# A spectral filter and a two-layer network on one core: all steps of the pieces placed anew, VectorE's half of the last operand sum at step 28 of its block in place of 21, and other steps for the loads of x

## The chip, the cores and the metric

The kernel runs on one core of a Trainium2 chip. The metric is the device time of one execution in microseconds; the time of a kernel is the median over its runs. Five engines run side by side, each with its own queue of instructions that it takes in order: TensorE (PE: matmuls; PEld: its weight loads), VectorE (DVE), ScalarE (ACT), GpSimd (POOL) and SyncE (SP). POOL and SP here mostly issue DMAs. Engines wait for each other by semaphores. One execution of the kernel before was profiled; all times of instructions below come from it.

## The reference

The first part multiplies each of 8 sequences (3008 positions, 256 channels) by a filter in the frequency domain; the second part is a two-layer network with a leaky rectifier whose slope is learned for each hidden unit.

```
batch, seq, dim = (8, 3008, 256)
n_tokens, d_model, d_ff = (24064, 256, 2048)
X = np.fft.rfft(x, axis=1)
F = (filt_r + 1j * filt_i)[None, :, :]
y = np.fft.irfft(X * F, n=x.shape[1], axis=1)
h = y.reshape(24064, 256) @ w_in
g = np.maximum(h, 0.0) + alpha * np.minimum(h, 0.0)
out = g @ w_out
```

## The kernel before

**The transform.** 3008 is 47 x 64. Each sequence b goes through four kinds of pieces, all built from matmuls with small constant matrices in fp16. The data are turned between them by way of DRAM, since the sums run over other indices.

- `load_x(b, c)`: four chunks c of x, two halves each, are loaded by DMAs that POOL issues (L170); they also convert to fp16. The tiles have four buffers.
- `piece_a` (16 a sequence): one matmul (L211), evicted by ScalarE to asb. `save_a` writes a chunk to a_dram (SP, L216) and `turn_a` reads it back turned to `at` (SP, L223).
- `piece_b` (12): two matmuls (L231), then two multiplications by the filter on VectorE: ww (L234) and uu (L235). Two DMAs from POOL then add ww, with its halves swapped, to uu (L237). These are the first kind of exchange.
- `piece_c` (12): two matmuls on uu (L249), evicted by ScalarE to v. `turn_c` writes a quarter of v to v_dram (SP, L258), `load_z` reads it back turned to zt (SP, L267).
- `piece_d` (16): four matmuls (L274), evicted to yT, the network's input.

Sequence 0 has its own way at the start (class `First`): its turns are done by TensorE, with `piece_t` (L352) in place of the way through v_dram. `neg` (L626) and `swapped` (L630) prepare the filter for the other sequences, and `combine` (L669 to L677) makes sums of the second layer's weights, in tw_s, which holds transform constants for sequence 0 before that.

**The network.** The tokens are cut into 48 blocks of 512 (some 384). For each block `up` runs 16 times: two matmuls with the first layer's weights (L498) into hps; after each second one ScalarE evicts a pair of hidden groups to gtb (L506), VectorE computes the negative part (L509, two) and adds it (L685, in `settle`). One `up` is a **step**, so block n covers the steps 16n to 16n + 15, and there are 768.

The second layer comes 17 steps later (LAG), spread evenly between the steps. Ordinary blocks use `eight` (L537): 64 matmuls of 256 columns. The blocks in FAST (the even ones from 8 on, here "split blocks") use `seven` (L559), a scheme with seven products of half-size operands in place of eight. It needs sums of quarters of gtb, made by `sums(w, h)` for half h of the hidden groups: w = 1 and 2 on VectorE to ss (L518, L520); w = 3 and 4 as accumulating DMAs from POOL onto gtb (L524), the second kind of exchange; w = 6 on VectorE, in place (L526). w = 6 with h = 1 and w = 4 with h = 0 are the two halves of the last operand sum; both are read by the last of the seven products. `late` holds VectorE's last additions and the stores, which SP issues (L467).

**What sets the order.** The order on every engine is written out by hand. The tables at the head of the file say at which step each piece is issued: STEPS_A to STEPS_D the pieces of sequences 4 to 7, FIRST those of 1 to 3, each plus p = 96 (b - 1); STEPS_T and STEPS_E the rest of sequence 0; STEPS_N `neg`; STEPS_F the move of a half of twi_s and then `swapped`; STEPS_K `combine`; STEPS_X and STEPS_Q the loads of x for the next sequence (STEPS_Q: two halves of four chunks, plus p). SUMS (TAIL near the end) holds (step in the block, w, h). BANKS says which of two PSUM banks each piece of the transform takes, in the order of issue. In a step the order is: late work, sums, pieces of the plan, `settle`, `up`, then the second layer's matmuls that are due:

```
for b, w, h in ahead.pop(step, ()):
    ...
    b.sums(w, h)
for fn, args in plan.pop(step, ()):
    fn(*args)
settle()
blk.up(j)
while todo and done < (step - LAG) / 16:
```

`turn_a` stands one step (sequences 1 and 2, in four parts) or four steps (the others) after the last `piece_a`; `turn_c` one step after each third `piece_c`.

Of the kernel before, what the change touches and what calls it, by code (L numbers as in the profile page):

```python
# [19 lines left out]
DFF = 2048  # L20
NH = 32
BANKS = (
    "010101010101010101010101010101001010010110010010101010101010100101001010010101010101010100101010"
    "101010101010101010101001010101001011010101011010110110101101010101010101101001011010101101010010"
    "101101010011010101101010101010101010110010101010101101001000101001010101010101010101010101010110"
    "101010101011010010010101101010101010101010101010101010010101101010110100100010100101010101010101"
    "01010101010101101010101101001110101010101010101010101010"
)
STEPS_A = (-84, -81, -77, -76, -65, -59, -58, -58, -56, -53, -52, -51, -50, -48, -46, -43)
STEPS_B = (-21, -15, 4, 6, 13, 21, 25, 27, 32, 40, 54, 55)  # L30
STEPS_C = (2, 10, 16, 19, 24, 33, 35, 46, 62, 63, 70, 70)
STEPS_D = (89, 89, 90, 91, 92, 94, 95, 98, 100, 101, 105, 113, 118, 125, 144, 147)
STEPS_T = (0, 0, 2, 2, 13, 17, 19, 21, 21, 35, 40, 43)
STEPS_E = (6, 6, 7, 11, 23, 27, 29, 29, 53, 54, 55, 56)
STEPS_N = (24, 29, 35, 40)
STEPS_F = (20, 16, 22, 28, 34)
STEPS_K = (118, 121, 128, 133, 144)
STEPS_X = ((20, 27, 42, 52), (107, 109, 113, 126))
STEPS_Q = (-28, -18, -8, -3, 1, 9, 15, 23)
FIRST = (  # L40
# [12 lines left out]
)  # L53
FAST = frozenset((8, 10, 12, 14, 16, 18, 20, 22, 24, 26, 28, 30, 32, 34, 36, 38, 40, 42, 43, 44, 45))
SUMS = ((9, 1, 0), (10, 3, 0), (16, 2, 0), (17, 1, 1), (17, 3, 1), (19, 2, 1), (20, 4, 0), (21, 6, 1))
TAIL = ((13, 1, 0), (13, 3, 0), (18, 1, 1), (18, 3, 1), (18, 2, 0), (18, 2, 1), (20, 4, 0), (21, 4, 1))
LAG = 17
AF = mybir.ActivationFunctionType
OP = mybir.AluOpType

# [41 lines left out]
def kernel(  # L102
# [514 lines left out]
    def put(step, fn, *args):  # L617
        plan.setdefault(step, []).append((fn, args))

    for i in range(12):  # L620
        ev = both[i % 2] if i < 4 else (on_dve, on_act)[i // 8]
        put(STEPS_T[i], f0.piece_t, 4 + i, ev)
        put(STEPS_E[i], f0.piece_d, 4 + i, ev)

# [6 lines left out]

    put(STEPS_F[0], lambda: nc.gpsimd.dma_start(out=twi_s[64:128], in_=twx_s[64:128]))
    for i in range(4):
        put(STEPS_F[1 + i], swapped, 6 * i, 6 * i + 6)
        put(STEPS_N[i], neg, 6 * i, 6 * i + 6)
    for b in range(1, NB):
        p = 96 * (b - 1)
        f = Fft(b)
        steps_a, steps_b, steps_c, steps_d = FIRST[b - 1] if b < 4 else (STEPS_A, STEPS_B, STEPS_C, STEPS_D)
        for i in range(16):  # L640
# [3 lines left out]
        if b + 1 < NB:  # L644
            for c in range(4):
                if b < 3:
                    put(STEPS_X[b - 1][c], load_x, b + 1, c)
                else:
                    for h in range(2):
                        put(p + STEPS_Q[2 * c + h], load_x, b + 1, c, (h,))  # L650
        quarters, later = (4, 1) if b < 3 else (1, 4)
# [27 lines left out]
    for n in range(5):  # L679
        put(STEPS_K[n], combine, n)  # L680
    owed = []
# [8 lines left out]
    for n, (p, t0, tn, _) in enumerate(blocks):  # L690
        old, blk = blk, Block(n, p, t0, tn)
        if blk.fast:
            for at, w, h in SUMS if n < 39 and n - 1 not in FAST else TAIL:
                ahead.setdefault(16 * n + at, []).append((blk, w, h))
        for j in range(16):
# [9 lines left out]
            blk.up(j)  # L705
            while todo and done < (step - LAG) / 16:
                try:
# [41 lines left out]
```

## Time and profile before

| what | us |
|---|---|
| median of 3 runs (777.71, 778.01, 780.72) | 778.01 |
| the profiled execution | 778.49 |
| its span, first to last instruction | 776.7 |
| TensorE busy (98% of the span) | 759.6 |
| VectorE busy (89%) | 691.0 |
| ScalarE busy (78%) | 606.1 |
| POOL busy (34%) | 264.7 |

The granted TensorE clock is 0.997 over the span. The span is cut into 40 equal slices (19.4 us each); TensorE is 90% busy or more in all but the first two and the last, and the DMA engines' share is given below it in tenths:

```profile
PE   7899999999999999999999999999999999999998
...
DMA  9996858666997679886797869966786645635642
```

A matmul's row is longer than its spacing to the next, because matmuls are pipelined. So a stop of TensorE is read from the starts of the rows: the start of a row, less the start of the row before it and that row's count times its spacing. In rows of the timeline, "xN" joins N instructions, and the brackets hold the idle time before the row and what ended it.

### The profile page before, as it was taken

What the parts mean: (1) busy time and instruction counts of PE and PEld (TensorE: products, weight loads), DVE (VectorE), ACT (ScalarE), POOL (GpSimd) and SP (SyncE); (2) the same over time, 40 slices, a digit from 0 to 9 for tenths busy, and PEclk for the clock granted to TensorE, in tenths of its full rate; (3) what the DMA queues carried; (4) which work ended last, traced back from release to release, by engine and by line L of the source; (5) the groups of instructions that cost most, each with busy time, mean ns of one, the idle gap of its engine ahead of it and who ended that gap; (6) DMA issues with size and microseconds to landing.
All of it is one profiled execution on the core that took longest, in us unless ns stands there. A gap on an engine that the chain in (4) does not pass through costs nothing.

```text
span 776.7 us, 18287 instructions
## 1 busy us (share of the span) xinstructions
PE 759.6 (98%) x6952; PEld 541.9 (70%) x6952; DVE 691.0 (89%) x1517; ACT 606.1 (78%) x902; POOL 264.7 (34%) x351
## 2 busy tenths in 40 slices
PE   7899999999999999999999999999999999999998
PEld 6756667666676767766677767767677777777776
DVE  3788996799999999999899999989999999989994
ACT  4687678888788887888878888788878777787773
POOL 6830641144234342353233422434222333103210
PEclk9999999999999999999999999999999999999999
DMA  9996858666997679886797869966786645635642
GB/s 181 191 191 185 163 110 209 185 130 138 192 201 153 125 162 189 207 151 129 162 196 151 156 136 178 210 134 131 161 191 153 127 86 103 167 84 105 129 96 68
DMA packets 112879, 118.74 MB, mean 153 GB/s; under 512 B 12616, under 2 KB 94296, under 8 KB 112792
## 3 DMA queue, kind: packets, MB, share of 16 engines
q0 software_dynamic: 32656, 47.99, 38.4%
q1 hardware_dynamic: 79992, 69.52, 33.7%
q8 instruction: 54, 0.88, 0.5%
q14 instruction: 33, 0.27, 0.1%
q10 hardware_dynamic: 144, 0.07, 0.0%
HBM read 56.06 MB, written 46.66 MB: 132 GB/s over the span
## 4 chain that ended last, share of the span: by engine, by line
PE 87%; DVE 4%; DMA 4%; ACT 3%; issue 1%; POOL 1%; SPq 1%; DVEq 0%; ACTq 0%; POOLq 0%
PE hps L498 38%; PE op L537 20%; PE op L559 16%; PE psF L211 3%; PE psF L274 3%; PE psF L249 2%; PE psF L231 2%; ACT gtb L506 2%; DMA twf_s<-c_twf 1%; DVE m L509 1%; DVE gtb L685 1%; DMA zt<-v_dram 1%; PE op L592 1%; DVE ww L234 1%; DVE uu L235 1%
## 5 line engine op out<-in xcount | busy, mean ns | idle before, releaser
L506 ACT ACTIVATE gtb<-hps 128x1024 f16<-128x1024 f32 (+1 forms) x384 | 385.9, 1005 | 110.5 <-PE hps L498 106.5
L498 PE MATMUL hps<-yT,win_s 128*128 128x512 f16 (+1 forms) x1536 | 449.2, 374 | 0.0
L509 DVE TENSOR_SCALAR m<-gtb,alm_s 128x512 f16<-128x512 f16 (+1 forms) x768 | 235.1, 348 | 45.4 <-ACT gtb L506 43.7
L685 DVE TENSOR_TENSOR gtb<-gtb,m 128x1024 f16<-128x1024 f16 (+1 forms) x384 | 260.9, 679 | 14.2
L537 PE MATMUL op<-wout_s,gtb 128*128 128x256 f16 x1600 | 243.1, 272 | 0.0
L237 POOL DMA_DIRECT2D uu<-ww x168 | 142.2, 1014 | 263.1 <-DVE uu L235 165.2
L537 PEld LDWEIGHTS <-gtb 128*128 128x128 f16 x1600 | 156.0, 98 | 104.6
L498 PEld LDWEIGHTS <-win_s 128*128 128x128 f16 x1536 | 136.7, 98 | 25.6 <-issue 2.5
L559 PEld LDWEIGHTS <-gtb 128*128 128x128 f16 x1680 | 114.3, 98 | 53.8 <-DMA gtb<-ss 1.0
L524 POOL DMA_DIRECT2D gtb<-gtb x42 | 40.5, 963 | 192.9 <-DVE ss L518 62.1
L559 PE MATMUL op<-wout_s,gtb 128*128 128x128 f16 x1008 | 85.1, 219 | 1.1 <-ACT gtb L506 0.6
L281 ACT ACTIVATE asb<-psF 96x512 f16<-96x512 f32 x112 | 65.1, 594 | 9.7 <-PE psF L211 8.4
L281 ACT ACTIVATE yT<-psF 128x376 f16<-128x376 f32 x120 | 56.2, 486 | 10.5 <-PE psF L274 9.3
L559 PEld LDWEIGHTS <-ss 128*128 128x128 f16 x672 | 47.1, 98 | 23.3
L170 POOL DMA_DIRECT2D xs<-in_x_dram x64 | 54.4, 1014 | 14.2 <-PE psF L211 13.4
L559 PE MATMUL op<-tw_s,gtb 128*128 128x128 f16 x672 | 58.1, 219 | 0.0
L559 PE MATMUL op<-tw_s,ss 128*128 128x128 f16 x672 | 58.0, 219 | 0.0
L234 DVE TENSOR_TENSOR ww<-psF,filts_s 128x512 f16<-128x512 f32 x84 | 57.4, 684 | 0.3 <-PE psF L231 0.2
L235 DVE TENSOR_TENSOR uu<-psF,filt_s 128x512 f16<-128x512 f32 x84 | 57.2, 681 | 0.0
L281 ACT ACTIVATE v<-psF 128x512 f16<-128x512 f32 x84 | 49.0, 598 | 7.8 <-PE psF L249 7.2
L211 PE MATMUL psF<-xs,wf_s 94*96 94x512 f16 x112 | 41.2, 380 | 1.4 <-ACT yT L281 0.4
L274 PE MATMUL psF<-wi_s,zt 96*128 96x94 f16 x504 | 39.4, 205 | 2.2 <-ACT yT L281 1.4
(86 smaller groups left out, 524.9 us busy)
## 6 DMA issues: line engine op xcount, KB each, us to landing
out_dram<-osb SPq DMA_DIRECT2D x127, 128.0 KB
xs<-in_x_dram POOLq DMA_DIRECT2D x64, 188.0 KB, 5.8
a_dram<-asb SPq DMA_DIRECT2D x28, 384.0 KB
uu<-ww POOLq DMA_DIRECT2D x168, 64.0 KB, 3.0
v_dram<-v SPq DMA_DIRECT2D x112, 96.0 KB
zt<-v_dram SPq DMA_DIRECT2D x28, 384.0 KB
gtb<-gtb POOLq DMA_DIRECT2D x42, 256.0 KB, 4.5
at<-a_dram SPq DMA_DIRECT2D x20, 384.0 KB
```

The costliest lines, as they stand in the source:

```text
L211: nc.tensor.matmul(ps[0:96], wf1_s, xs[:, o : o + 512], start=True, stop=True)
L234: nc.vector.tensor_mul(ww, px, filts_s[:, 2 * kp : 2 * kp + 2])
L235: nc.vector.tensor_mul(uu, px, filt_s[:, 2 * kp : 2 * kp + 2])
L237: nc.gpsimd.dma_start(out=uu[o : o + 64], in_=ww[64 - o : 128 - o], accum_op=OP.add)
L274: nc.tensor.matmul(ps[:, m], self.zt[g][:, 4 * mh + m, dh * 128 : dh * 128 + 128], wi3_s, start=True, stop=True)
L281: nc.scalar.activation(o, i, AF.Copy)
L498: nc.tensor.matmul(self.hps[:, j % 2, 0:tn], win_s[:, kt, j * 128 : (j + 1) * 128], yT[:, kt, self.t0 : self.t0 + tn], start=(kt == 0), st ...
L506: nc.scalar.activation(g, hs, AF.Copy)
L509: nc.vector.tensor_scalar(ms[:, i], g[:, i], 0.0, a, OP.min, OP.mult)
L537: nc.tensor.matmul(op[:, si % 2], self.pair(k // 2)[:, k % 2, 128 * si : 128 * si + 128], wout_s[:, k], start=(k == 0), stop=(k == 15))
L559: nc.tensor.matmul(acc[:, 128 * i : 128 * i + 128], x[:, k, 128 * i : 128 * i + 128], b[:, k], start=first and k + i == 0, stop=k == 7, sk ...
L685: nc.vector.tensor_add(g, g, ms)
```

## The change

Only the tables at the head of the file change. No instruction is added or taken away on any engine. The pieces, the loads of x, `neg`, `swapped` and `combine` get other steps, the sums of the split blocks other places in the block (the last one, w = 6 with h = 1, step 28 in place of 21), and BANKS follows the new order. In the diff the lines of BANKS are left out.

```diff
--- before.py
+++ after.py
@@ -20,41 +20,41 @@
 DFF = 2048
 NH = 32
 BANKS = (
...
 )
-STEPS_A = (-84, -81, -77, -76, -65, -59, -58, -58, -56, -53, -52, -51, -50, -48, -46, -43)
-STEPS_B = (-21, -15, 4, 6, 13, 21, 25, 27, 32, 40, 54, 55)
-STEPS_C = (2, 10, 16, 19, 24, 33, 35, 46, 62, 63, 70, 70)
-STEPS_D = (89, 89, 90, 91, 92, 94, 95, 98, 100, 101, 105, 113, 118, 125, 144, 147)
-STEPS_T = (0, 0, 2, 2, 13, 17, 19, 21, 21, 35, 40, 43)
-STEPS_E = (6, 6, 7, 11, 23, 27, 29, 29, 53, 54, 55, 56)
-STEPS_N = (24, 29, 35, 40)
-STEPS_F = (20, 16, 22, 28, 34)
-STEPS_K = (118, 121, 128, 133, 144)
-STEPS_X = ((20, 27, 42, 52), (107, 109, 113, 126))
-STEPS_Q = (-28, -18, -8, -3, 1, 9, 15, 23)
+STEPS_A = (-83, -81, -78, -76, -66, -64, -58, -58, -55, -52, -51, -50, -50, -47, -44, -44)
+STEPS_B = (-23, -11, 4, 8, 10, 23, 26, 30, 34, 42, 48, 55)
+STEPS_C = (2, 11, 18, 23, 24, 35, 37, 51, 60, 63, 70, 70)
+STEPS_D = (89, 89, 90, 92, 93, 94, 94, 97, 101, 103, 104, 112, 117, 125, 136, 150)
+STEPS_T = (0, 0, 2, 2, 13, 17, 19, 21, 21, 39, 44, 45)
+STEPS_E = (6, 6, 10, 11, 23, 24, 27, 30, 48, 52, 58, 58)
+STEPS_N = (24, 33, 36, 57)
+STEPS_F = (31, 11, 24, 29, 36)
+STEPS_K = (108, 115, 121, 121, 135)
+STEPS_X = ((22, 44, 53, 82), (98, 103, 126, 134))
+STEPS_Q = (-42, -39, -28, -9, -7, -6, 7, 8)
 FIRST = (
-    ((8, 10, 15, 16, 16, 17, 19, 20, 22, 22, 24, 25, 26, 28, 28, 30),
-     (41, 41, 45, 45, 49, 54, 58, 63, 65, 65, 71, 72),
-     (48, 50, 52, 58, 60, 62, 69, 70, 71, 73, 77, 80),
-     (94, 94, 95, 95, 96, 102, 102, 105, 105, 107, 108, 111, 119, 120, 120, 129)),
-    ((-34, -28, -26, -21, -20, -18, -18, -17, -16, -14, -14, -10, -9, -8, -7, 0),
-     (13, 13, 16, 18, 27, 31, 37, 39, 44, 48, 55, 61),
-     (25, 29, 30, 38, 41, 42, 45, 47, 56, 64, 65, 77),
-     (93, 93, 95, 95, 97, 100, 104, 106, 107, 110, 112, 119, 121, 122, 124, 129)),
-    ((-75, -69, -65, -62, -61, -60, -60, -57, -54, -48, -46, -43, -42, -38, -37, -37),
-     (-11, -9, 0, 5, 10, 18, 25, 32, 40, 41, 49, 54),
-     (5, 6, 16, 22, 29, 31, 36, 46, 58, 68, 72, 72),
-     (91, 92, 92, 95, 95, 95, 99, 100, 101, 103, 106, 113, 119, 125, 149, 149)),
+    ((5, 9, 9, 16, 16, 17, 19, 20, 22, 22, 24, 25, 26, 26, 28, 29),
+     (39, 40, 41, 47, 50, 53, 54, 63, 64, 66, 70, 72),
+     (47, 50, 53, 57, 60, 63, 68, 69, 70, 74, 76, 80),
+     (94, 94, 95, 95, 96, 99, 103, 103, 104, 106, 106, 109, 119, 121, 121, 122)),
+    ((-34, -29, -25, -21, -20, -18, -18, -17, -16, -12, -12, -11, -9, -9, -5, -4),
+     (11, 12, 16, 18, 28, 34, 37, 39, 44, 49, 54, 61),
+     (23, 29, 32, 37, 43, 46, 51, 52, 57, 64, 66, 78),
+     (93, 94, 94, 95, 97, 100, 105, 107, 108, 109, 112, 116, 118, 119, 121, 131)),
+    ((-75, -69, -66, -64, -62, -60, -58, -57, -54, -48, -47, -43, -42, -38, -37, -35),
+     (-15, -6, -5, 0, 10, 17, 22, 26, 33, 40, 42, 49),
+     (5, 7, 14, 17, 24, 26, 30, 36, 60, 61, 67, 72),
+     (91, 91, 93, 93, 94, 98, 99, 101, 102, 103, 105, 111, 122, 125, 150, 152)),
 )
 FAST = frozenset((8, 10, 12, 14, 16, 18, 20, 22, 24, 26, 28, 30, 32, 34, 36, 38, 40, 42, 43, 44, 45))
-SUMS = ((9, 1, 0), (10, 3, 0), (16, 2, 0), (17, 1, 1), (17, 3, 1), (19, 2, 1), (20, 4, 0), (21, 6, 1))
-TAIL = ((13, 1, 0), (13, 3, 0), (18, 1, 1), (18, 3, 1), (18, 2, 0), (18, 2, 1), (20, 4, 0), (21, 4, 1))
-LAG = 17
+SUMS = ((11, 1, 0), (13, 3, 0), (14, 2, 0), (18, 1, 1), (18, 3, 1), (20, 2, 1), (21, 4, 0), (28, 6, 1))
+TAIL = ((13, 1, 0), (18, 3, 0), (19, 1, 1), (19, 2, 0), (20, 2, 1), (23, 3, 1), (23, 4, 0), (25, 4, 1))
+LAG = 17.0
 AF = mybir.ActivationFunctionType
 OP = mybir.AluOpType
```

More of the change, by code (lines that the diff above doesn't have):

```diff
@@ L22 @@
 BANKS = (
[L23 to L27, printed above, removed]
-)
-STEPS_A = (-84, -81, -77, -76, -65, -59, -58, -58, -56, -53, -52, -51, -50, -48, -46, -43)
@@ L40 @@
-FIRST = (
[12 rows of a table removed]
+    "010101010101010101010101010101010101010110010010100101010101010101101010101010101001010010101010"
+    "101010101010101010101001001010101101011010100101010010100101001010100101001010110101010101010010"
+    "101010010100101010010101010101010101101001101010101101011011010101010110101001010101010101010010"
+    "100101010101101001001010101010110101010101010101010100101001010101011010010010101010101101010101"
+    "01010101010100101001010110101101010101010101010101010101"
+)
+STEPS_A = (-83, -81, -78, -76, -66, -64, -58, -58, -55, -52, -51, -50, -50, -47, -44, -44)
```

## The prediction

> **What bounds the kernel now.** I read the page first: busy shares and the chain that ended last.
>
> ```profile
> PE 759.6 (98%) x6952; PEld 541.9 (70%) x6952; DVE 691.0 (89%) x1517; ACT 606.1 (78%) x902; POOL 264.7 (34%) x351
> ...
> PE 87%; DVE 4%; DMA 4%; ACT 3%; issue 1%; POOL 1%; SPq 1%; DVEq 0%; ACTq 0%; POOLq 0%
> ```
>
> TensorE is the bound and runs almost without a break. The change has the same instructions on every engine, in another order, so TensorE's own work stays; all that can be won or lost are its stops. The list of waits hardly shows them (most have 0.2 to 0.6 us each), so I went through the timeline of PE and compared the start of each row with where the row before should have ended. Usual spacings come from undisturbed rows (two 512-column matmuls 0.43 us, four 256-column ones 0.44, 128 columns 0.057 each, 94 columns 0.044 each).
>
> ```profile
> 79.38 0.60 PE L537 MATMUL op<-wout_s,gtb 128*128 128x256 f16 x4
> 80.45 0.39 PE L352 MATMUL psF<-id,v 128*96 128x128 f16 x2 [0.47 <-DVE uu L235]
> ...
> 89.33 0.60 PE L537 MATMUL op<-wout_s,gtb 128*128 128x256 f16 x4
> 90.52 0.39 PE L249 MATMUL psF<-uu,twi_s 128*128 128x256 f16 x2 [0.59 <-DMA uu<-ww]
> ...
> 188.74 0.50 PE L559 MATMUL op<-wout_s,gtb 128*128 128x128 f16 x6
> 189.69 0.23 PE L559 MATMUL op<-wout_s,gtb 128*128 128x128 f16 x1 [0.46 <-DVE gtb L685]
> ...
> 374.44 0.50 PE L274 MATMUL psF<-wi_s,zt 96*128 96x94 f16 x8
> 375.35 0.38 PE L211 MATMUL psF<-xs,wf_s 94*96 94x512 f16 x1 [0.41 <-ACT yT L281]
> ...
> 505.63 0.44 PE L559 MATMUL op<-tw_s,gtb 128*128 128x128 f16 x5
> 506.70 0.28 PE L559 MATMUL op<-wout_s,gtb 128*128 128x128 f16 x2 [0.62 <-ACT gtb L506]
> ```
>
> First pair: 79.38 + 0.44 = 79.82, the next row starts at 80.45, so 0.63 us are lost. So read, the stops over 0.1 us are 3.6 us in sum between 36 and 65 us (the crowded start) and 7.2 us after it: 0.63 at 79.8, 0.75 at 89.8, 0.56 at 110.8, 0.17 and 0.54 at 148 to 150, 0.61 at 189.1, 0.44 at 241.6, 0.56 and 0.19 at 321 to 322, 0.56 at 374.8, 0.43 at 499.4, 0.78 at 505.9, and 1.0 in seven small ones. That is all this change has to win after the start.
>
> The merged chain says what was late at some of them:
>
> ```profile
> 77.92 0.56 DVE filt_s L626
> ...
> 188.44 0.60 DVE tw_s L677
> 189.03 0.61 DVE gtb L685
> ...
> 493.68 6.09 DMA zt<-v_dram
> ```
>
> A step below is one `up` (two matmuls at L498); there are 768, some 0.95 us each ((725.0 - 38.8) / 720).
>
> **The change, part by part.** Each entry: the stop, the old and the new steps, and what I take.
>
> - 79.8 (step 43): L352 of the last `piece_t` waits for VectorE, which ran the `neg` of step 40 (0.56 us, the first chain row) and two `piece_b` just before. That is the fourth `neg`; it goes to 57, the `piece_b` to 39, 40, 41, the `piece_t` to 45. Cause gone: -0.63.
> - 89.8 (step 52): `piece_c` 2 waits for the landing of `uu<-ww`, seven steps after its `piece_b` (45 to 52). Now twelve (41 to 53): -0.75.
> - 110.8 (step 71): `piece_c` 8 comes six steps after its `piece_b`, now six again (64 to 70): 0.
> - 148 to 150 (step 111): `piece_d` waits for a bank that VectorE frees after `uu`. The first two `piece_b` of sequence 2 go from 109, 109 to 107, 108, this `piece_d` from 111 to 109: the distance shrinks while the pair is spread. Between 0 and -0.71; I take -0.2.
> - 189.1 (step 147): the down matmul waits for L685, behind the fifth `combine` at step 144 (0.60 us in the chain). They move to 108 to 135; the products that need them begin at 145. -0.61.
> - 241.6: an eviction to osb waited for a store's landing; the order on SP changes all around it. 0 to -0.44; -0.2.
> - 321 and 322 (step 287): three `piece_d` of one sequence stand on one step and ScalarE evicts all three. Now they stand at p + 93, 94 and 98 (285, 286, 290), at most two a step. -0.75.
> - 374.8 (step 341): two `piece_d` and a `piece_a` on one step; now 342 and 344, the `piece_a` on 340. -0.56.
> - 499.4 and 505.9: transfers. zt took 6.09 us, and w4 of block 28 landed after its use. The queue of POOL there:
>
> ```profile
> 496.53 0.97 POOL L524 DMA_DIRECT2D gtb<-gtb  x1 [3.23 <-PE op L559]
> 498.95 1.65 POOL L237 DMA_DIRECT2D uu<-ww  x2 [1.46 <-DVE ss L520]
> 500.01 1.51 POOL L524 DMA_DIRECT2D gtb<-ss  x1
> 500.59 2.54 POOL L170 DMA_DIRECT2D xs<-in_x_dram  x3
> ```
>
> The exchange w4 (`gtb<-ss`, put at 468) stands behind two `uu<-ww` of a `piece_b` put at 465. Now w4 is at 469 and that `piece_b` also at 469, and sums go ahead of the plan in a step: w4 is issued ahead of both, 500.01 - 498.95 = 1.06 us earlier, but w3 before it is put one step later. 0 to -0.78; -0.6. For zt, the load of x put at 462 (it was issued at 492.16, inside zt's time) is gone from there: 0 to -0.43; -0.4.
> - small ones: -0.2 of 1.0.
>
> Sum of gains: 0.63 + 0.75 + 0.2 + 0.61 + 0.2 + 0.75 + 0.56 + 0.6 + 0.4 + 0.2 = 4.9.
>
> **Loads of x.** p is a multiple of 96 and a split block starts at a multiple of 32, so phases modulo 32 tell the order on POOL. Before: x at 1, 4, 9, 14, 15, 23, 24, 29, exchanges at 10, 17, 20: two loads stand between exchanges and one just ahead. Now: x at 4, 7, 8, 22, 23, 25, 25, 26, exchanges at 13, 18, 21: none between, the nearest ahead by five steps (4.8 us, against 5.8 us median to landing). Nothing on TensorE waits for x: the tightest is chunk 3, from step 8 to the `piece_a` at 96 - 50 = 46. What it may cost is the other queue: the loads at -42 and -39 now lie around `turn_a` at -40, whose four transfers of 384 KB must land by `piece_b` at -23, 17 steps or 16 us on; 1.5 MB at the 200 GB/s of the fuller slices are 7.9 us, and two loads of 188 KB do not use up the rest. Cost 0, at most one wait like 0.75 us in each of four sequences, 3.0.
>
> [...]
>
> **The sum at step 28.** VectorE's add (L526) is no shorter, and the wait it could bring is on PE, where the last product reads its result.
>
> ```profile
> L526 DVE TENSOR_TENSOR gtb<-gtb,ss x16: 683/684/687, 193.4 to 650.6; 128x1024 f16<-128x1024 f16 x16
> ```
>
> From the trace, these adds start 0.8 to 3.4 us after the first matmul of their step (VectorE runs that far behind), and end 6.3 to 9.3 us before the matmul that needs them. Steps 21 to 28 take 5.5 to 7.2 us. In the tight blocks (14, 16, 22, 28, 34) the difference is 0.6 to 0.8 us; but VectorE is 3.6 to 3.9 us behind at step 22 there and 1.3 to 2.5 at 28, which gives back 1.4 to 2.4. Some 2 us are left: cost 0. If it were late, all 16 blocks would pay up to the 0.61 us of the row at 189.69: 9.8. If it frees VectorE at the crowded step 21, up to 0.6 is won. The other sums move by one or two steps against needs at step 24 or later; w3's POOL issue gets two steps after w1 instead of one, so the uu transfers behind it on POOL wait less.
>
> **New stops.** `piece_b` 0 of sequence 1 goes from 41 to 39 while its `turn_a` moves from 31 to 30: its quarter of at is issued by step 36 now. 0 to 0.75 (the wait at 89.8); 0.3. `piece_c` 7 and 8 both have six steps now (7 was seven): 0 to 0.56; 0.3. Some clump of evictions in a plan with this many places: 0.4, the size of the one at 241.6. Start (36 to 65 us): T, E and first A are as crowded as before; between -1 and +1, 0. BANKS follows the new order and costs nothing itself. Together +1.0.
>
> Net -4.9 + 1.0 = -3.9. The profiled execution took 778.49 us around a span of 776.7; that gives 774.6. The median of the runs is 0.48 lower: 778.01 - 3.9 = 774.1.
>
> **Rivals.**
>
> 1. The stops move rather than go: as many new clumps and late landings as old ones. For it: hundreds of steps move, and only some twelve were stops. Against: each named stop has its own cause that the new numbers take apart. 778 +- 0.6.
> 2. Nearly every stop after 65 us goes: 778.0 - 7.2 = 770.8, with some of the start too at best. Against: 6-step distances remain.
> 3. Slower: the add at step 28 is late. Place: last product of the 16 split blocks; price 9.8 against the 3.9 won, so 778.0 + 5.9 = 783.9 if all pay; it decides once VectorE runs over some 4 us behind at step 28 (6.4 blocks paying 0.61 us give back all the 3.9). Against: 1.3 to 2.5 us there now.
> 4. The loads of x do not get out of the way but into another: `turn_a` late, +3.0, or 777.1; and if zt is caught too, 780.
>
> **How the numbers follow.** Forecast 0.56, rival 2 0.15, rival 1 0.17, rival 3 0.07, rival 4 0.05. A change under 0.5% (3.9 us) counts as none here. The forecast lies on that bound (774.1): 0.31 of its chance to faster, 0.25 to the middle. Faster 0.31 + 0.15 = 0.46; same 0.25 + 0.17 + 0.02 = 0.44; slower 0.07 + 0.03 = 0.10. Range 770.8 (rival 2) to 778.6 (rival 1 with its margin); the forecast's own is 772 to 776.
>
> **What would show it.** Right: no stop near 80, 90, 189, 322, 375 us; w4's transfers landing before the last product; the uu to L249 wait only near 107 us; L526 ending about 2 us ahead of its use. Wrong: PE waiting for L526 (DVE gtb) in many blocks; L231 waiting for at<-a_dram; more than 5 us of new stops after 65 us.

## The result, and the profile after

The changed kernel takes 782.5 us at the median of 13 runs (779.2 to 785.7), the kernel before 778.9 beside it (13 runs, 777.7 to 783.6). The ratio is 1.0039, with a 95% interval of 1.0026 to 1.0053: slower by some 3 us, where 774.1 was forecast. The profiled execution of the changed kernel took 782.59 us, its span is 780.7.

From the page of the changed kernel, the busy shares and the chain that ended last:

```profile
PE 757.9 (97%) x6952; PEld 540.2 (69%) x6952; DVE 686.7 (88%) x1517; ACT 606.2 (78%) x902; POOL 264.2 (34%) x351
...
PE 86%; DMA 6%; DVE 3%; ACT 2%; POOL 1%; issue 1%; ACTq 0%; POOLq 0%; DVEq 0%
```

TensorE has the same 6952 matmuls in a span that is 4 us longer, and DMA's share of the chain went from 4% to 6%. The list of waits of the changed kernel already names the place:

```profile
PE psF L231 <- DMA out_dram<-osb: 3.9, 2, 2.0
...
PEld L231 <- DMA at<-a_dram: 2.3, 1, 2.3
```

L231 is `piece_b`, which reads `at`. The timeline of PE shows the three places (start, length, row, idle before it and what ended it):

```profile
304.27 0.60 PE L537 MATMUL op<-wout_s,gtb 128*128 128x256 f16 x4
305.85 0.38 PE L231 MATMUL psF<-at,twf_s 128*128 128x256 f16 x2 [0.98 <-issue]
...
394.58 0.60 PE L537 MATMUL op<-wout_s,gtb 128*128 128x256 f16 x4
397.05 0.38 PE L231 MATMUL psF<-at,twf_s 128*128 128x256 f16 x2 [1.87 <-DMA out_dram<-osb]
...
489.23 0.60 PE L537 MATMUL op<-wout_s,gtb 128*128 128x256 f16 x4
491.85 0.39 PE L231 MATMUL psF<-at,twf_s 128*128 128x256 f16 x2 [2.02 <-DMA out_dram<-osb]
```

Read by the starts as before, these are stops of 1.14, 2.03 and 2.18 us, each ahead of the first `piece_b` of sequence 4, 5 or 6. The brackets name a store, or nothing; the semaphore that ended the wait serves several of SP's transfers in turn. The landing of a transfer is the last update of its semaphore ahead of the next transfer on it. So read, the last part of `at` lands at 396.91, just ahead of 397.05, and for the other two at 305.76 and 491.81, each within 0.15 us of the row of `piece_b`.

The fourth large stop is at step 89. Timeline of the changed kernel, all engines:

```profile
128.55 0.60 PE L537 MATMUL op<-wout_s,gtb 128*128 128x256 f16 x4
...
129.23 1.08 ACT L281 ACTIVATE asb<-psF 96x512 f16<-96x512 f32 x2 [3.00 <-PE op L537]
130.20 1.51 ACT L506 ACTIVATE gtb<-hps 128x768 f16<-128x768 f32 x2
131.04 0.55 DVE L509 TENSOR_SCALAR m<-gtb,alm_s 128x384 f16<-128x384 f16 x2 [3.57 <-ACT gtb L506]
131.06 0.48 PE L498 MATMUL hps<-yT,win_s 128*128 128x384 f16 x2 [1.91 <-ACT gtb L506]
```

and the chain that ended last, around it:

```profile
119.68 9.46 DMA a_dram<-asb
```

ScalarE idles 3.0 us ahead of an eviction to asb. The tile has two buffers, and the write of the older one to a_dram (`save_a` of sequence 2) took 9.46 us. Everything behind that eviction on ScalarE's queue waits too, L506 among it, and TensorE stops for 2.07 us. Then the clock halves; the table of stretches (length, PE busy, granted clock, DMA share, GB/s) says:

```profile
core 0: us, PE busy (x), PEclk, DMA share, GB/s
60.00:132.00 72.00, 68.65 (x504) 1.00 0.67 147
132.00:135.50 3.50, 3.50 (x15) 0.51 0.91 257
135.50:300.00 164.50, 163.56 (x1433) 1.00 0.77 165
```

3.41 us at half clock cost about 1.7 us more. The half clock is not the whole loss: 5 of the 13 runs of the changed kernel have a granted clock of 0.999 or more, and their median is 781.9 us, that of the other eight 782.7.

What the change was to remove is mostly removed. Stops over 0.15 us after 65 us in the changed kernel, apart from these four and the slow stretch, are 0.23 at 77, 0.92 at 107.7, 0.23 and 0.32 at 148 to 150, 0.48 and 0.56 at 230 to 232. Those near 80, 90, 189, 242, 321, 375, 499 and 506 us are gone.

### The profile page after: what moved, and what is told of

It is laid out like the page before. It is cut to its first block, busy times and chain, and to the rows that moved or that the text cites. A ratio compares the mean times of both kernels' runs of the same rounds, so it can differ in the third digit from the quotient of the medians.

```text
span 780.7 us, 18289 instructions
## 1 busy us (share of the span) xinstructions
PE 757.9 (97%) x6952; PEld 540.2 (69%) x6952; DVE 686.7 (88%) x1517; ACT 606.2 (78%) x902; POOL 264.2 (34%) x351
## 4 chain that ended last, share of the span: by engine, by line
PE 86%; DMA 6%; DVE 3%; ACT 2%; POOL 1%; issue 1%; ACTq 0%; POOLq 0%; DVEq 0%
PE hps L498 38%; PE op L537 20%; PE op L559 16%; PE psF L211 3%; PE psF L274 3%; PE psF L231 2%; PE psF L249 2%; DMA a_dram<-asb 2%; ACT gtb L506 1%; DMA gtb<-ss 1%; DMA filt_s<-in_filt_r_dram 1%; DVE m L509 1%; DVE gtb L685 1%; DMA out_dram<-osb 1%; PE op L592 1%
## 5 line engine op out<-in xcount | busy, mean ns | idle before, releaser
L506 ACT ACTIVATE gtb<-hps 128x1024 f16<-128x1024 f32 (+1 forms) x384 | 385.9, 1005 | 107.8 <-PE hps L498 102.9
L537 PE MATMUL op<-wout_s,gtb 128*128 128x256 f16 x1600 | 244.1, 273 | 0.0
L537 PEld LDWEIGHTS <-gtb 128*128 128x128 f16 x1600 | 156.5, 98 | 105.2 <-issue 0.7
L559 PEld LDWEIGHTS <-gtb 128*128 128x128 f16 x1680 | 114.3, 98 | 52.6 <-DMA gtb<-ss 0.6
L524 POOL DMA_DIRECT2D gtb<-gtb x42 | 47.6, 1134 | 120.7 <-DVE ss L518 49.9
L559 PE MATMUL op<-wout_s,gtb 128*128 128x128 f16 x1008 | 84.9, 219 | 0.4 <-DMA gtb<-ss 0.4
L281 ACT ACTIVATE asb<-psF 96x512 f16<-96x512 f32 x112 | 64.6, 595 | 15.3 <-PE psF L211 11.8
L281 ACT ACTIVATE yT<-psF 128x376 f16<-128x376 f32 x120 | 56.3, 488 | 10.4 <-PE psF L274 9.1
L559 PEld LDWEIGHTS <-ss 128*128 128x128 f16 x672 | 47.1, 98 | 23.3
L281 ACT ACTIVATE v<-psF 128x512 f16<-128x512 f32 x84 | 49.8, 600 | 10.9 <-PE psF L249 10.0
L559 PE MATMUL op<-tw_s,gtb 128*128 128x128 f16 x672 | 58.1, 219 | 0.0
L559 PE MATMUL op<-tw_s,ss 128*128 128x128 f16 x672 | 58.0, 219 | 0.0
L170 POOL DMA_DIRECT2D xs<-in_x_dram x64 | 46.8, 978 | 11.9 <-PE psF L211 10.2
L211 PE MATMUL psF<-xs,wf_s 94*96 94x512 f16 x112 | 40.1, 382 | 1.5 <-DVE zt L284 1.2
```

Of the source, the lines that this page charges most:

```text
L211: nc.tensor.matmul(ps[0:96], wf1_s, xs[:, o : o + 512], start=True, stop=True)
L281: nc.scalar.activation(o, i, AF.Copy)
L506: nc.scalar.activation(g, hs, AF.Copy)
L537: nc.tensor.matmul(op[:, si % 2], self.pair(k // 2)[:, k % 2, 128 * si : 128 * si + 128], wout_s[:, k], start=(k == 0), stop=(k == 15))
L559: nc.tensor.matmul(acc[:, 128 * i : 128 * i + 128], x[:, k, 128 * i : 128 * i + 128], b[:, k], start=first and k + i == 0, stop=k == 7, sk ...
```

## The experiments

All are compared with the kernel before on the same chip. e1 to e4, e5 to e8 and e9 to e12 ran on three different chips, so between them the ratios count more than the times. Each diff is against the changed kernel unless it says otherwise. Where a piece is moved, BANKS is put in the new order so that each piece keeps its bank. For transfers of `at` I give times from the start of step p - 43 (the write of the last chunk of asb follows it); the first `piece_b` is at step p - 23 or p - 21.

| run | median, us | ratio to before (95%) |
|---|---|---|
| the change | 782.52 | 1.0039 (1.0026 to 1.0053) |
| e1 loads of STEPS_Q back | 778.75 | 0.9988 (0.9968 to 1.0008) |
| e2 first `piece_b` at -21 | 779.14 | 0.9993 (0.9979 to 1.0008) |
| e3 loads of STEPS_X back | 779.69 | 0.9999 (0.9982 to 1.0017) |
| e4 both tables of loads back | 775.80 | 0.9953 (0.9935 to 0.9971) |
| e5 e4, VectorE's half sum at 21 | 776.27 | 0.9957 (0.9941 to 0.9973) |
| e6 before with the new loads | 788.37 | 1.0096 (1.0067 to 1.0126) |
| e7 e3, loads behind `piece_b` | 778.83 | 0.9992 (0.9977 to 1.0007) |
| e8 e4, three `piece_c` later | 777.25 | 0.9969 (0.9955 to 0.9984) |
| e9 one load of STEPS_X back | 779.35 | 1.0008 (0.9990 to 1.0026) |
| e10 e2 and e3 | 776.77 | 0.9973 (0.9956 to 0.9990) |
| e11 e4 and e2 | 776.80 | 0.9969 (0.9955 to 0.9983) |
| e12 e7 but for sequence 4's loads | 776.69 | 0.9971 (0.9956 to 0.9987) |

**e1: the loads of STEPS_Q as before.**

```diff
-STEPS_Q = (-42, -39, -28, -9, -7, -6, 7, 8)
+STEPS_Q = (-28, -18, -8, -3, 1, 9, 15, 23)
```

> The changed kernel with the eight loads of x of sequences 5 to 7 (STEPS_Q) back at -28, -18, -8, -3, 1, 9, 15, 23; all else as changed. Theory A (these loads run ahead on POOL into the time of turn_a and make at late): the three stops before the first piece_b of sequences 4, 5 and 6 (1.14, 2.03, 2.19 us; 5.4 in all) fall under 1 us in sum, at lands about 1.9 us earlier, and the median falls by 4 to 5 us, to about 778. Theory B (the first piece_b, two steps earlier, is what does it): the stops stay within a third of their size, the median falls by under 1.5 us.

(The loads that STEPS_Q places are those for sequences 4 to 7.) Measured: 3.8 us less than the change (4.0 by the ratios), at the foot of the 4 to 5 expected. The three stops are under 0.15, 0.28 and under 0.15 us; `at` lands at 16.4, 18.3 and 17.5 us for sequences 4, 5 and 6, in place of 18.8, 20.1 and 20.2. Nothing but these loads was moved, so theory A holds. The profile still has the stop at step 89 (2.42 us, half clock behind it) and one of 2.1 us at 231.7, where the change had 0.56.

**e2: the room.**

```diff
-STEPS_B = (-23, -11, 4, 8, 10, 23, 26, 30, 34, 42, 48, 55)
+STEPS_B = (-21, -11, 4, 8, 10, 23, 26, 30, 34, 42, 48, 55)
```

> The changed kernel with the first piece_b of sequences 4 to 7 back at -21 in place of -23; the loads of x stay as changed. Theory A: at lands as late as in the changed kernel (19.6 us after the start of step 341 for sequence 5), two steps (1.9 us) more of room leave 0 to 0.3 us of each stop, so this alone also gives most of it back: the median falls by 3 to 5 us. If that happens and e1 gives as much, lateness and room share the cause. If the stops merely move by two steps and keep their size, something else than room decides.

Measured: 3.4 us less than the change. For sequences 4 and 5 `at` lands as late as in the change (18.9 and 20.6 us; for sequence 5 step p - 23 starts at 18.5 us, and p - 21 at 20.9 with its stop); for sequence 6 it lands at 18.9, 1.2 us earlier than in the change. Of the three stops one of 0.5 us is left. So lateness and room share the cause: in the changed kernel `at` came 1.8 to 2.3 us later than before (18.8, 20.1 and 20.2 us), `piece_b` wanted it two steps (some 1.9 us) earlier, and the kernel before had only 2.0 to 2.9 us between the two (landing at 16.9, 17.8 and 18.0 us against step p - 21 at 19.9, 20.0 and 20.0). The 3.4 us are not all from here: in this profile the stop at step 89 is 1.2 us without half clock, though nothing was edited there.

What made `at` late is seen in POOL's timeline. In the changed kernel, around the start of step 341 (376.8 us):

```profile
377.35 1.34 POOL L170 DMA_DIRECT2D xs<-in_x_dram  x1
381.34 1.70 POOL L237 DMA_DIRECT2D uu<-ww  x2 [2.64 <-DVE uu L235]
382.41 1.70 POOL L170 DMA_DIRECT2D xs<-in_x_dram  x2
```

and in the kernel before (step 341 begins at 375.6 us):

```profile
379.41 3.52 POOL L237 DMA_DIRECT2D uu<-ww  x4 [4.20 <-DVE uu L235]
382.26 1.21 POOL L170 DMA_DIRECT2D xs<-in_x_dram  x1
```

The loads at -42, -39 and -28 are put at steps 342, 345 and 356 of sequence 5, but the third is issued at 383.06, in step 347, nine steps ahead of its place: nothing that it waits for is missing, and the two exchanges in front of it on POOL (381.34) wait no longer. So three loads (which land at 386.0, 388.2 and 390.4 us) are in flight when the four transfers of `at` are issued (383.9 to 386.3), where in the kernel before there was one (it lands at 391.0, the transfers are issued from 381.5 to 383.3).

**e3 and e9: step 89.**

```diff
-STEPS_X = ((22, 44, 53, 82), (98, 103, 126, 134))
+STEPS_X = ((20, 27, 42, 52), (107, 109, 113, 126))
```

> The changed kernel with the loads of x for sequences 2 and 3 (STEPS_X) back at 20, 27, 42, 52 and 107, 109, 113, 126. Theory C (the load put at 82 in place of 52 lies with those at 98 and 103 ahead of save_a of sequence 2, whose write to a_dram took 9.5 us in place of 5.5; ScalarE waits 3.0 us for an asb buffer and holds up the step): the stop of 2.07 us at step 89 and the half clock of 3.4 us right behind it (about 1.7 us lost) go, the median falls by 2 to 4 us. Rival: the write is late because save_a itself moved (steps 84 and 85 in place of 82 to 86), then the stop stays.

Measured: 2.8 us less than the change; no stop at step 89, no half clock there, the write of asb takes 4.9 us. `save_a` stayed at its new step, so the rival falls. In this profile the stops at L231 are smaller too (0.67, 1.32 and 1.53 us) with nothing edited there, so not all of the 2.8 us need come from step 89. POOL's timeline shows which loads lie beside that write, in the changed kernel:

```profile
115.35 2.78 POOL L170 DMA_DIRECT2D xs<-in_x_dram  x4
119.32 1.01 POOL L170 DMA_DIRECT2D xs<-in_x_dram  x2 [1.19 <-PE psF L211]
```

and in e3:

```profile
117.38 1.78 POOL L170 DMA_DIRECT2D xs<-in_x_dram  x2
```

The six are the halves of the chunks put at 82, 98 and 103, issued in steps 75 to 79: here too POOL ran ahead, by up to 24 steps, and only the last pair waited, 1.2 us for a `piece_a` (L211) to be done with its buffer. The kernel before has four loads there (put at 107 and 109) and a write of 5.5 us.

e9 puts back only the last load for sequence 2:

```diff
-STEPS_X = ((22, 44, 53, 82), (98, 103, 126, 134))
+STEPS_X = ((22, 44, 53, 52), (98, 103, 126, 134))
```

> The changed kernel with one entry of STEPS_X put back: the last chunk of x for sequence 2 at step 52 in place of 82. Theory C in its narrow form: that one chunk (two loads issued at 115.4 and 115.9 us) is what makes the write of asb late (9.5 us), so the stop at step 89 falls from 2.1 to under 0.5 us and the median by 2 to 3.5 us, as in e3. If the loads at 98 and 103 do it, the stop keeps over 1 us and the median falls by under 1 us.

Measured: 3.2 us less than the change (0.31% by the ratios, e3 0.40%; the intervals overlap), four loads lie beside the write, which takes 7.9 us, and the stop is 0.62 us. So in these two profiles the one chunk is most of the stop, though only a part of the write's delay: with the loads of sequence 3 as before too the write takes 4.9 us. e9's 0.62 lies over the 0.5 that was expected, but no half clock follows it.

**e4: both tables of loads as before.** (The diffs of e1 and e3 together.)

> The changed kernel with both tables of loads of x (STEPS_Q, STEPS_X) as before. Theories A and C together: all four large stops gone, 5.4 + 2.1 + 1.7 = 9 us less at best, some given back at the exchanges (the stops of 0.43 and 0.78 us near 500 us may return): 774 to 777, below the kernel before. If the changed steps of the other pieces are what costs, it stays above 779.

Measured: 775.8, ratio 0.9953: 0.86% under the change, and below the kernel before. PE at the same place as above, without a stop, in the profile of e4:

```profile
391.54 0.60 PE L537 MATMUL op<-wout_s,gtb 128*128 128x256 f16 x4
391.97 0.38 PE L231 MATMUL psF<-at,twf_s 128*128 128x256 f16 x2
```

The four rows of L537 take 0.43 us and L231 follows at once. The stops over 0.15 us after 65 us are 3.8 us in e4, 7.0 in the kernel before. Separately the two tables gave back 0.51% and 0.40%, together 0.86%: as far as these runs can tell, they add.

**e5: VectorE's half sum.** e4 with

```diff
-SUMS = ((11, 1, 0), (13, 3, 0), (14, 2, 0), (18, 1, 1), (18, 3, 1), (20, 2, 1), (21, 4, 0), (28, 6, 1))
+SUMS = ((11, 1, 0), (13, 3, 0), (14, 2, 0), (18, 1, 1), (18, 3, 1), (20, 2, 1), (21, 4, 0), (21, 6, 1))
```

> The kernel of e4 (both tables of loads of x as before) with VectorE's half of the last operand sum back at step 21. Theory D (the add at step 28 has about 2 us of room and costs nothing): within 1 us of e4's 775.8, the adds end 6 us or more ahead of their use in place of 1.8 to 2.7. If step 28 helps by clearing VectorE at the crowded step 21, this is slower than e4 by up to 3 us, with stops of PE behind DVE in the split blocks; if step 28 hurts, it is faster by over 1 us.

Measured: 776.3 against 775.8, with ratios of 0.9957 and 0.9953: no difference that these runs can tell. In e5 the 16 adds end 7.4 to 9.8 us ahead of the matmul that reads them, in the changed kernel and in e4 1.8 to 2.7, as worked out. The part of the change that stands first in its name is worth nothing that can be told here; each ratio is known to some 1.3 us either way.

**e6: the new loads in the old order.** The kernel before with

```diff
-STEPS_X = ((20, 27, 42, 52), (107, 109, 113, 126))
-STEPS_Q = (-28, -18, -8, -3, 1, 9, 15, 23)
+STEPS_X = ((22, 44, 53, 82), (98, 103, 126, 134))
+STEPS_Q = (-42, -39, -28, -9, -7, -6, 7, 8)
```

> The kernel before with the changed kernel's two tables of loads of x, and nothing else. If the loads alone are the loss (theory A without the room, and C): at lands 1.9 us later, which just uses up the 1.8 to 2.3 us of room that this kernel has, so the stops at L231 are 0 to 0.5 us each, and the stop at step 89 comes with its 2 us, half clock behind it: 2 to 5 us slower than before. If the loads of x at their new places are harmless with the old steps, no more than 1 us.

Measured: 0.96% slower, about 7.5 us: more than expected. (The profiled execution, 792.2 us, is the slowest of the six.) Of the stops at L231, one is 1.2 us; the stop at step 89 became 0.78 and 1.33 us at steps 88 and 93; and two large ones came that were not expected: 2.3 us at 491 us (L249) and, with half clock behind it,

```profile
515.59 0.44 PE L559 MATMUL op<-tw_s,gtb 128*128 128x128 f16 x5
518.62 0.28 PE L559 MATMUL op<-wout_s,gtb 128*128 128x128 f16 x2 [2.59 <-DMA gtb<-ss]
```

the stop before step 480 that the kernel before had with 0.78 us, now 2.75. The exchange w4 took 9.1 us, and 6.6 in the kernel before. Three loads right behind it on POOL and zt on SP are no difference: the kernel before has both. What differs in the two traces is that POOL issued w3, two uu transfers and w4 between 507.87 and 509.49 us, in 1.6 us, where the kernel before took 3.5 (496.53 to 500.01). Whether that is why w4 landed later was not tried. So the loads at -9, -7 and -6 are no help to the exchanges with the old order either; in the changed kernel w4 goes out ahead of the two uu transfers and took 6.6 us.

**e7 and e12: loads where POOL can't run ahead.** e3 with

```diff
-STEPS_Q = (-42, -39, -28, -9, -7, -6, 7, 8)
+STEPS_Q = (-22, -21, -20, -9, -7, -6, 7, 8)
```

> The kernel of e3 (loads of sequences 2 and 3 as before) with the first three loads of STEPS_Q at -22, -21, -20, right behind the first piece_b, in place of -42, -39, -28; the other five as changed (-9, -7, -6, 7, 8). POOL then cannot run ahead with them past the exchanges of that piece_b. Theory A: no load of x lies in turn_a's time, at lands 1 to 3 us earlier than in e4, no stop at the first piece_b of sequences 4 to 6, about e4's time, 775 to 777.5. If bunching six loads between -22 and -6 costs the exchanges there, stops at L249 or L559 around steps 280, 375, 470 of 0.5 to 2 us each and 777 to 780.

Measured: 778.8, not the 775 to 777.5. Where the loads do stand behind the first `piece_b`, `at` lands at 14.6, 15.7 and 15.0 us, 1 to 3 us ahead of e4, and no stop is left. But for sequence 3 the first `piece_b` is at -15 and not -23, which I had overlooked, so there the loads stand ahead of it. POOL and PE in e7:

```profile
201.22 2.22 POOL L170 DMA_DIRECT2D xs<-in_x_dram  x3
...
214.35 0.60 PE L537 MATMUL op<-wout_s,gtb 128*128 128x256 f16 x4
217.33 0.38 PE L231 MATMUL psF<-at,twf_s 128*128 128x256 f16 x2 [2.38 <-DMA at<-a_dram]
217.55 0.59 PE L498 MATMUL hps<-yT,win_s 128*128 128x512 f16 x2
...
218.36 1.06 PE L498 MATMUL hps<-yT,win_s 128*128 128x512 f16 x2
```

Loads put at 170 to 172 were issued in steps 161 and 162, with the transfers of `at` of sequence 3 (from 203.3 us), and PE stopped for 2.5 us. The last row shows the half clock: the same two matmuls take 1.06 us and not 0.59. e12 gives these loads their old steps:

```diff
-                        put(p + STEPS_Q[2 * c + h], load_x, b + 1, c, (h,))
+                        put(p + ((-28, -18, -8, -3, 1, 9, 15, 23) if b == 3 else STEPS_Q)[2 * c + h], load_x, b + 1, c, (h,))
```

> The kernel of e7 with the loads issued while sequence 3 is in hand (those for sequence 4) at the steps before, -28 to 23; for the later ones still -22, -21, -20, -9, -7, -6, 7, 8. In e7 the loads put at 170 to 172 were issued at step 161 and 162, with turn_a of sequence 3, whose at landed in step 176 and stopped PE for 2.5 us with half clock behind it. Theory A: that stop goes with its half clock, 2.5 + 1.7 us at best, the median falls by 2.5 to 4 us to 775 to 776.5. If the stop stays, it is not the loads.

Measured: 776.7, 2.1 us less than e7 (0.21% by the ratios, whose intervals overlap), under the 2.5 expected and 0.2 over the range for the time. The stop at step 176 and its half clock are gone. In the traces, the cause has now been moved to a place where it wasn't, and taken away again. e12 is not faster than e4: where e4 has 1.4 us of stops around 230 us (0.48, 0.51, 0.38), e12 has 2.0, and it has another 1.7 near 321 us. Most of that is two waits of L559 for exchanges that took 8.7 and 9.7 us, 7.4 and 8.2 in e4. The loads at -22 to -20 are in the way here: the exchange w3 (`gtb<-gtb`) that POOL issues right behind the three of them took 10.7 to 11.7 us in sequences 4 to 6, the same one in e4, with at most one load and that behind it, 3.6 to 5.8.

**e8, e10, e11: better versions?**

e8 is e4 with `piece_c` 6, 7, 8 of sequence 1 at 69, 70, 71 in place of 68, 69, 70.

> The kernel of e4 with three piece_c of sequence 1 one step later (numbers 6, 7 and 8 at 69, 70, 71 in place of 68, 69, 70), so that two of them have seven steps and not six after their piece_b. The stop at step 69 (1.06 us in e4) waits for a uu transfer: it should fall to 0 to 0.3 us and the median by 0.5 to 1 us, to about 775. If the transfer is late because POOL issues it late behind others, the stop moves by a step and keeps most of its size.

Measured: 777.3, not faster than e4. The stop stayed at 1.17 us and one of 0.85 came behind it. Their releaser is another: the brackets no longer name uu but ScalarE's eviction of v (L281 of the changed kernel, which is L268 in e8's file), and pieces that follow each other now use the same bank (BANKS reads 1001100010 there, where it read 1001010010), which would explain it. Another of 1.8 us at 120.6 waits for a uu transfer of 6.6 us; e4 has 0.39 there. Why that transfer is longer was not tried. One more of 1.8 us came at 230.8, where e4 has 0.37.

e10 is the edits of e2 and e3 together.

> The changed kernel with the first piece_b of sequences 4 to 7 back at -21 and STEPS_X as before; STEPS_Q stays as changed. If lateness of at and room add up as a plain difference, giving room is as good as taking the loads away: stops at the first piece_b of at most 0.5 us each, no stop at step 89, 775.5 to 777, beside e4's 775.8. If the loads of x near turn_a also cost elsewhere, 777 to 779.

Measured: 776.8, stops at L231 of 0.4 us at most, as expected if lateness and room subtract.

e11 is e4 with the first `piece_b` at -21.

> The kernel of e4 with the first piece_b of sequences 4 to 7 at -21. at lands 0.5 to 1.5 us ahead of step -23 in e4, so its stops there are already gone; two steps more of room give nothing on the path: within 1 us of 775.8. Faster by over 1 us would say that runs other than the profiled one still stop there; slower, that the later transfers of this piece_b delay something else.

Measured: 776.8, 1.0 us from e4. The lowest ratio is that of e4, 0.5% below the kernel before; the intervals of e5, e8, e10, e11 and e12 overlap with its own.

## Why the prediction was wrong

- **The bound.** Right: no work of TensorE changed, and the stops decide.
- **The gains.** Right for all but small parts. Of the stops that were forecast to go, those at 79.8, 89.8, 189.1, 241.6, 374.8, 499.4 and 505.9 us are gone, those at 321 to 322 but for 0.11; the pair at 148 to 150 fell from 0.71 to 0.55 (0.2 had been taken). The start, taken as 0 within 1 us, has 4.4 us of stops for 3.6. w4 of block 28 does go out right behind w3 and ahead of the uu transfers, and lands at 510.56 for a use at 511.00.
- **New stops.** Those forecast were about right, 1.6 us in sum for the 1.0 taken: 0.23 at `piece_b` 0 of sequence 1 (0.3 taken), 0.92 for 0.56 at `piece_c` 7 and 8 (0.3 more taken), 0.48 and 0.56 near 230 us (one of 0.4 taken). With the old tables of loads, e4, the ratio is 0.9953, that is 3.7 us less than 779.3: the forecast of -3.9 is about what the change does without its loads of x. That it comes so close is in part luck: in e4's profile the stops after 65 us fall by 3.2 us (7.0 to 3.8), and the 0.4 at zt was credited to the load put at 462, which is back there in e4 while the stop is gone all the same (e1 and e5, with that load back too, have 0.41 and 0.44 there).
- **The step that failed: "Loads of x", and its "Cost 0, at most one wait like 0.75 us in each of four sequences, 3.0".** It failed in three places. First, it read the phases of the loads as times. On POOL they are only an order, and the queue ran up to nine steps ahead, so that -42, -39 and -28 all met `turn_a`. Nor did the other new phases do what was claimed for them: near w4 of block 28 the loads put at 471, 473 and 474 were issued in steps 473 to 475, and those of the kernel before, put at 472, 477 and 481, in steps 473 and 474. Second, it gave `at` "17 steps or 16 us" for 7.9 us of transfer. The transfers are issued only some 5 to 7 us after step p - 43, when the write before them has landed; from the first issue to the last landing they took 11.2 to 11.8 us in the kernel before, not 7.9, and 13.0 to 14.0 in the changed one. The kernel before had 2.0 to 2.9 us to spare, not eight; the landings could have been read from the trace. Third, the bound: a wait for a DMA of 0.75 us elsewhere does not bound this one. Measured 1.14, 2.03 and 2.18, with 0.51% or 4.0 us in the time (e1 against the change). This is rival 4, which had 0.05: its "`turn_a` late" is what happened, and its 777.1 was too low. Both of its signs came: L231 waits for `at<-a_dram`, and there are more than 5 us of new stops after 65 us.
- **What was left out.** The new place of the last chunk for sequence 2 in STEPS_X, 82 for 52, was in the diff and is named nowhere in the working. The only test made of a load was when x is needed, not whose transfers it lies beside. It cost 2.07 us at step 89 and 1.7 by the half clock in the profiled run, 0.40% or 3.1 us in the time with the rest of its table (e3), most of the stop by that one chunk (e9). The two chunks moved from 107 and 109 to 98 and 103 joined it there.
- **The other queue.** The working let the loads beside `turn_a` cost nothing ("two loads of 188 KB do not use up the rest"). With three loads in flight on POOL's queue and not one, SP's four transfers of `at`, with the same bytes, landed 1.8 to 2.3 us later.
- **Rival 3.** Rightly put low: 1.8 to 2.7 us were left at step 28, the 2 us of the working, and moving the add back changes nothing that can be told (e5).
- **Rivals 1 and 2.** Neither. The old stops went, and the large new ones come from the loads and go with them (e4), so the stops did not merely move; and even in e4 3.8 us of stops remain, so rival 2's 770.8 is not reached.

## What to carry to other kernels

The step at which a DMA stands in a program is an order, not a time (here POOL issued loads up to nine steps ahead of their places, and at step 79 up to 24): find in the trace when the queue issues it and what is in front of it that holds it back. Before a transfer is moved, list what else is in flight where it will land, and read the room of each of those transfers (landing to first use) from the trace; here the kernel before had 2.0 to 2.9 us there, and of two edits that each took some 2 us, either one without the other left stops of at most 0.28 (e1) or 0.5 us (e2), and both together 1.14, 2.03 and 2.18. Account for every entry of a diff of numbers, also those of work that nothing is waiting for.

## What the runs showed of the hardware

In the profile of the changed kernel a stretch of half clock of 3.41 us (132.10 to 135.51 us, granted clock 0.50) followed the stop of 2.07 us. From there to 780.6 us the granted clock is 1.00, so the stops of 2.03 and 2.18 us at 395 and 490 had none. In the profile of the kernel before a stretch of 3.41 us lies in the start (21.70 to 25.12), and in both profiles another is under way at the end (from 780.63 and from 776.05). In the experiments, the stops of 2.42 (e1), 2.5 (e7) and 2.75 us (e6) were followed by half clock, those of 2.1 (e1), 2.3 (e6) and 2.6 us (e9) were not; e9's granted clock over the whole span is 0.999, where one stretch of 3.41 us would leave 0.998. So in these runs the length of a stop alone did not tell whether it cost 1.7 us more, and what else decides it was not shown.
